# Second pair's 1/rms by bit shift and refinements on VectorE, whole-tile output stores, a split last tile

## Chip, core and metric

The kernel runs on one core of a Trainium2 chip. The metric is the device time of one execution in microseconds (us), as the median of several runs. The engines are named as the profile names them: PE (TensorE matmul), PEld (its weight loads), DVE (VectorE), ACT (ScalarE), POOL (GpSimd), SP (SyncE, which here issues nearly all DMAs; its queue is SPq).

## What is computed

Memory-compressed attention for 8 batches x 8 heads x 576 positions x 64 dimensions with 32 memory slots, and behind it an RMS norm and a gated feed-forward layer over 4608 tokens (512 -> 1536 -> 512).

```python
a = softmax(phi, axis=2)                          # 576 x 32 per head
k_m, v_m = a.T @ k, a.T @ v                       # 32 x 64 per head
x = softmax(q @ k_m.T / sqrt(64)) @ v_m           # then heads side by side: 4608 x 512
xn = x / sqrt(mean(x * x, axis=-1) + 1e-6) * rms_g
g = xn @ w_gate
out = (g * sigmoid(g) * (xn @ w_val)) @ w_out
```

q, k, v and phi are float32, the three weight matrices arrive as 8-byte floats, and the output is float32, 4608 x 512.

## The kernel before

The 8 batches are worked in 4 pairs. The kernel never forms x @ w: it multiplies v_m into the weights first (`vp`, tokens then enter through the 32-slot attention weights), so that one unit of work is small. Where float32 accuracy is wanted from a matmul, an operand is split into a high part and a low remainder (`xh`/`xl`, `ath`/`atl`, `hh`/`hl`, `oh`/`ol`) and three products are added: high x high, high x low, low x high. The high part is a cast on ACT, the remainder a subtraction on POOL or DVE.

**First stage (about 0 to 130 us).** For each batch phi is exponentiated, k and v are compressed (`kvp`), turned and normalized; for pairs 0 and 1 q is loaded, scores `S` and their softmax `a` are formed. `x_steps` then prepares the tokens of a pair: `a` is turned (`tp`, `at`), the norm's sum of squares comes from a small product with the v_m Gram matrix (`xp`, `ssq`, lines 275 to 293), and `fin` (lines 302 to 328) makes 1/rms from it, a 128x9 tile `rinv`. `fin` has two ways, chosen by `PRM["LN"]`: a pair whose number is below LN takes ln and exp on ACT (lines 312 and 313) and one refinement step on DVE; the others take an integer shift and a multiply-add on DVE (lines 316 and 319) and three refinement steps (lines 324 to 326, each three 128x9 instructions). With LN=2 pairs 0 and 1 go by ln and exp, pairs 2 and 3 by the shift. Behind `fin` come three groups of steps per pair: `rinv` is spread over partitions by PE (`rp`, line 238, for pair 1 in a buffer of the two that `po` uses too), DVE multiplies it into `at` (line 246), and ACT and POOL split `at` into `ath` and `atl` (lines 266 and 267). For pair 1 these last steps are put off into the second stage (`x_tail`).

**Second stage (from about 130 us).** 48 steps; the first 24 belong to pairs 0 and 1, the last 24 to pairs 2 and 3. Step i makes `vp` (12 matmuls, line 546) and splits it into `xh`, `xl` (lines 558 and 559), then the gate and value products `pg` and `pv` for its two batches and for two groups of token tiles (line 586), Silu of `pg` on ACT (`sg`, line 594), the product `hf` on DVE (line 595) and its split `hh`, `hl` (lines 613 and 614). After every second step (`out_steps`), for each of 9 token tiles t, 6 matmuls of 128x512 make `po` (line 1120); the first unit copies it into `acc` on ACT (line 1125), later ones add it on DVE (line 1128), and after the last unit the tile is stored by two DMAs of 64 rows each, one per batch of the pair (line 1132). So there are two bursts of stores: pairs 0 and 1 in the middle of the kernel (about 484 to 545 us) and pairs 2 and 3 at its end. During the first 24 steps the weights are converted from 8-byte floats with integer instructions on DVE (lines 413 to 443, `ex` and `mi`) and helpers on ACT and POOL, and pairs 2 and 3 get their attention. In the second half `vp` of pairs 2 and 3 is formed for both at once (`vq`, line 1059), split into `sh` and `sl` (lines 1083 and 1084) and sent in pieces of 32 rows to the places of `xh` and `xl` by DMA (line 1102); `sl` and `sh` get new values only when those DMAs have read them.

**Order.** Every step has a due time from the table `PRM` (in units of a first-stage clock, later in steps). All steps are sorted by it and written out; a scheduler with a model of the engines then fixes the order of each engine's queue. Each engine works through its queue in order. ACT must hold the table that has the function it is to run: an ACT_TABLE_LOAD stands wherever the next function needs another one. In the trace a load stands ahead of Silu, of ln and of exp wherever the function before was another of the three, save for pair 0's norm, which needs none.

Of the kernel before, what the change touches and what calls it, by code (L numbers as in the profile page):

```python
# [8 lines left out]
F32 = mybir.dt.float32  # L9
# [4 lines left out]
ALU = mybir.AluOpType  # L14
# [19 lines left out]
    POST=[-0.351, 1.753, 3.361, 9.334, 15.437, 18.292],
    P1=4.425,
    PREP=[4.415, 7.26, 7.26, 7.26, 20.861],
    PD=[1.16, 10.918, 7.968, 18.215, 7.667, 0.808],
    EXP=[-5.547, 10.093, -0.851, 3.808, 8.158, 5.953],
    ES=1.713,
    PH=[10.189, 16.336, 43.784, 73.222, 98.48, 135.656],  # L40
    S_AT=[32.811, 49.336, 51.299, 66.888, 103.621, 110.389, 116.081, 123.226],
    KD=[-25.933, -115.469, -42.204, -7.345, -6.094, -11.232, -0.175, -2.269, -27.578, -16.354, -20.47, -8.311,
        -12.025, -12.235, -27.337, -21.619, -19.41, -32.053, -14.0, -25.731, -11.785, -19.02, -8.155, -10.419,
# [37 lines left out]
    XN=[-0.287, -0.179, -0.049, 0.046, 0.258, 0.5, 0.652, 0.838, 0.858],
    LV=[19.704, 21.121, 20.046, 22.191],
    VD=[42.193, 5.807, 18.26, 22.229],
    U=[[-1.593, -1.385, -1.385, -1.17, -0.987, -0.894], [-1.558, -1.498, -1.292, -1.023, -1.023, -0.981],
        [-1.863, -1.411, -1.203, -0.927, -0.927, 0.553]],
    RL=[-1.987, -3.598, -5.966],
# [22 lines left out]
def kernel(  # L109
# [87 lines left out]
    def x_steps(pr, a, psum_t, psum_x, fetch=None, psum_r=None):  # L197
# [104 lines left out]
        def fin():  # L302
# [53 lines left out]
    raw, wsplit, wosplit, halves = {}, {}, {}, {}  # L356
# [39 lines left out]
    urgent = []  # L396
# [110 lines left out]
    NS = (NP // G) * NU * G * 2  # L507
    vw, vp_, whole, hsplit, accs, fourth = {}, {}, {}, {}, {}, []

    def mixed(i):  # L510
        return i >= NS // 2 + 2 * G

    def where(i):

        ps_, r = divmod(i, NU * G * 2)
        u, r = divmod(r, G * 2)
        pi, f = divmod(r, 2)
        if mixed(i):
            pi, f = f, pi
        return ps_, u, ps_ * G + pi, 2 * u + f  # L520
# [103 lines left out]
    with ExitStack() as c1:  # L624
# [3 lines left out]
        ps = c1.enter_context(tc.tile_pool(name="ps1", bufs=2, space=PSUM, reuse_waits="tile"))  # L628
# [412 lines left out]
    ps = ctx.enter_context(tc.tile_pool(name="ps2", bufs=2, space=PSUM, reuse_waits="tile"))  # L1041
# [64 lines left out]
    def out_steps(i):  # L1106

        ps_, u, pr, j = where(i)

        def f(t):  # L1110
            def g():
                gi = 0 if t < GROUPS[1][0] else 1
                po = ps.tile([P, 512], F32, tag="o", name=f"po{i}_{t}")
                m = 0
                for s in (i - 2 if mixed(i) else i - 1, i):
                    hh, hl = hsplit[s, gi]
                    oh, ol = wosplit[ps_ * NJ + where(s)[3]]
                    tt = t - GROUPS[gi][0]
                    for l, r in ((hh, oh), (hh, ol), (hl, oh)):
                        nc.tensor.matmul(po, l[:, tt, :], r, start=(m == 0), stop=(m == 5))  # L1120
                        m += 1
                key = pr % G, t
                if u == 0:
                    accs[key] = sb.tile([P, 512], F32, tag=f"acc{key[0]}_{t}", name=f"acc{pr}_{t}")
                    nc.scalar.copy(accs[key], po)
                else:
                    urgent.append(
                        nc.vector.tensor_tensor(out=accs[key], in0=po, in1=accs[key], op=ALU.add).ins  # L1128
                    )
                if u == NU - 1:  # L1130
                    for b in range(2):
                        nc.sync.dma_start(
                            out[(2 * pr + b) * S:(2 * pr + b + 1) * S].rearrange("(p c) d -> p c d", c=NT)[:, t, :],
                            accs[key][64 * b:64 * b + 64, :],
                        )
            return g
        return [f(t) for t in range(NT)]
# [119 lines left out]
    for i in range(NS):  # L1257
        ps_, u, pr, j = where(i)
# [21 lines left out]
    for a, (kind, n, p, e) in enumerate(items):  # L1280
        c = convert(kind, n)
# [46 lines left out]
```

## Time and profile before

| | |
|---|---|
| median of 3 runs | 855.59 us (855.2, 855.59, 857.08) |
| the profiled execution, its time | 850.64 us |
| its span, first to last instruction | 848.9 us (1.7 us less) |
| mean granted TensorE clock | 0.989 |
| PE busy | 812.3 us, 96% of the span |
| DVE, ACT, POOL busy | 537.0, 403.7, 322.9 us |
| chain that ended last | PE 74%, DVE 9%, DMA 5%, ACT 3%, issue 3%, POOL 3%, SPq 2% |
| output stores | 72 DMAs of 128.0 KB, 2.4 us to landing |

A row of the timeline gives the start in us from the span's beginning, the duration, the engine, the line, the operation, out<-in with shapes, how many instructions are merged into it, and in square brackets how long the engine stood idle before it and what released it. A row of a window table gives the length of the window, then for each engine its busy time in it with the number of instructions, and the granted PE clock, the DMA share and GB/s at the end. The profiled execution is 4.95 us shorter than the median of the timed runs; the profile does not say why.

### The profile page before, as it was taken

Reading aid. Unit: us, or ns where it says so; the run is one execution under the profiler, and the core shown is the slowest. Engines: PE = TensorE matmul, PEld = TensorE weight load, DVE = VectorE, ACT = ScalarE, POOL = GpSimd, SP = SyncE. Lnnn points to the kernel's source line nnn. Section 1 sums busy time; section 2 is a strip of 40 time slices with the busy share of each in tenths; the row PEclk is TensorE's granted clock in tenths of the full one; section 3 lists DMA queues with packets and bytes.
Section 4 is the critical chain, followed back from the end, with each engine's and each line's share of the span. In section 5 each row is a group of like instructions: output and inputs, shape, how many; then the busy total and the mean of one; then the engine's idle time right before and its main releaser. Section 6 shows DMA issues by size and latency. Waiting matters only on the chain.

```text
span 848.9 us, 16232 instructions
## 1 busy us (share of the span) xinstructions
PE 812.3 (96%) x6234; PEld 731.9 (86%) x6234; DVE 537.0 (63%) x940; ACT 403.7 (48%) x731; POOL 322.9 (38%) x279
## 2 busy tenths in 40 slices
PE   5989997999999999999999989999999999999997
PEld 4878886889989889988989888899999999999996
DVE  5697868876678898979889546312354454444434
ACT  2767647687565465656454423354333223232220
POOL 3565746734444563643544512411212122121220
PEclk9889999999999999999999999999999999999999
DMA  9997525545343543743534567806736357264437
GB/s 335 364 383 271 201 72 152 149 117 153 115 119 96 167 124 78 189 132 104 150 111 130 176 144 198 239 15 168 180 94 179 77 149 199 59 153 88 100 100 174
DMA packets 99493, 131.62 MB, mean 155 GB/s; under 512 B 42324, under 2 KB 61784, under 8 KB 99416
## 3 DMA queue, kind: packets, MB, share of 16 engines
q1 hardware_dynamic: 99416, 130.59, 54.6%
q8 instruction: 49, 0.80, 0.4%
q14 instruction: 28, 0.23, 0.1%
HBM read 73.93 MB, written 31.46 MB: 124 GB/s over the span
## 4 chain that ended last, share of the span: by engine, by line
PE 74%; DVE 9%; DMA 5%; ACT 3%; issue 3%; POOL 3%; SPq 2%; ACTq 0%; POOLq 0%; DVEq 0%
PE po L1120 31%; PE pg L586 14%; PE pv L586 14%; PE vp L546 3%; PE vq L1059 3%; PE kvp L787 2%; SPq L1102 1%; DVE xl L559 1%; DMA kv_0x<-in_k_dram 1%; DVE mi L438 1%; DVE ex L413 1%; DVE ex L416 1%; PE S L1199 1%; PE xp L280 1%; ACT xh L558 1%
## 5 line engine op out<-in xcount | busy, mean ns | idle before, releaser
L614 POOL TENSOR_TENSOR hl<-hf,hh 128x512 fp32r<-128x512 f32 (+1 forms) x86 | 124.5, 1449 | 285.7 <-ACT hh L613 285.6
L1128 DVE TENSOR_TENSOR acc<-po,acc 128x512 f32<-128x512 f32 x180 | 123.5, 688 | 124.2 <-PE po L1120 123.5
L1120 PE MATMUL po<-oh,hh 128*128 128x512 f32 x387 | 154.1, 399 | 4.5 <-DVE at L246 1.9
L1120 PE MATMUL po<-ol,hh 128*128 128x512 f32 x387 | 153.3, 396 | 0.5 <-DMA ol<-od 0.5
L1120 PE MATMUL po<-oh,hl 128*128 128x512 f32 x387 | 151.5, 391 | 0.0
L595 DVE TENSOR_TENSOR hf<-pv,sg 128x320 f32<-128x320 f32 (+1 forms) x188 | 83.4, 452 | 88.4 <-PE pv L586 64.3
L594 ACT ACTIVATE sg<-pg 128x320 f32<-128x320 f32 (+1 forms) x188 | 76.6, 410 | 123.4 <-PE pg L586 115.2
L586 PE MATMUL pg<-ath,xh 128*128 128x320 f32 (+1 forms) x376 | 85.9, 301 | 3.9 <-ACT sg L594 3.6
L1120 PEld LDWEIGHTS po<-oh,hh 128*128 128x128 f32 x387 | 73.0, 189 | 16.9 <-DVE at L246 2.1
L1120 PEld LDWEIGHTS po<-oh,hl 128*128 128x128 f32 x387 | 73.0, 189 | 16.1
L586 PE MATMUL pg<-ath,xl 128*128 128x256 f32 (+1 forms) x376 | 83.8, 297 | 0.7 <-DMA xl<-sl 0.7
L613 ACT CAST hh<-hf 128x512 fp32r<-128x512 f32 (+1 forms) x86 | 57.4, 672 | 55.2 <-DVE hf L595 37.6
L586 PE MATMUL pv<-ath,xl 128*128 128x256 f32 (+1 forms) x376 | 82.9, 296 | 0.0
L586 PE MATMUL pg<-atl,xh 128*128 128x256 f32 (+1 forms) x376 | 82.9, 297 | 0.0
L586 PE MATMUL pv<-ath,xh 128*128 128x320 f32 (+1 forms) x376 | 82.2, 298 | 0.4 <-DVE hf L595 0.3
L586 PE MATMUL pv<-atl,xh 128*128 128x256 f32 (+1 forms) x376 | 81.6, 296 | 0.0
L1120 PEld LDWEIGHTS po<-ol,hh 128*128 128x128 f32 x387 | 73.1, 189 | 9.0 <-DMA ol<-od 0.7
L462 POOL TENSOR_TENSOR w<-mi,ex 128x512 f32<-128x512 f32 x34 | 43.9, 1290 | 84.8 <-ACT mi L450 54.6
L586 PEld LDWEIGHTS pg<-ath,xh 128*128 128x128 f32 x376 | 62.6, 189 | 9.2 <-ACT sg L594 4.3
L559 DVE TENSOR_TENSOR xl<-vp,xh 64x1024 fp32r<-64x1024 f32 x48 | 58.5, 1219 | 16.4 <-ACT xh L558 15.6
L586 PEld LDWEIGHTS pv<-ath,xh 128*128 128x128 f32 x376 | 61.6, 189 | 3.6 <-DVE hf L595 0.9
L586 PEld LDWEIGHTS pg<-ath,xl 128*128 128x128 f32 x376 | 62.2, 190 | 2.8 <-DMA xl<-sl 0.9
(163 smaller groups left out, 1519.7 us busy)
## 6 DMA issues: line engine op xcount, KB each, us to landing
xh<-sh SPq DMA_DIRECT2D x96, 128.0 KB, 3.7
xl<-sl SPq DMA_DIRECT2D x80, 128.0 KB, 3.1
out_dram<-acc SPq DMA_DIRECT2D x72, 128.0 KB, 2.4
raw<-in_moe_w_gate_dram SPq DMA_DIRECT2D x12, 512.0 KB, 4.0
raw<-in_moe_w_val_dram SPq DMA_DIRECT2D x12, 512.0 KB, 3.8
raw<-in_moe_w_out_dram SPq DMA_DIRECT2D x12, 512.0 KB, 4.0
wd<-whl SPq DMA_DIRECT2D x24, 256.0 KB, 3.8
whl<-wd SPq DMA_DIRECT2D x12, 512.0 KB, 5.3
```

What stands on the lines that cost most here:

```text
L462: (nc.gpsimd if on_pool else V).tensor_tensor(out=d["w"], in0=m, in1=ex, op=ALU.mult)
L546: nc.tensor.matmul(vp[:, cc, e, :], lhs(l), r[:, 2 * cc + e, :], start=(n == 0), stop=(n == 2),)
L559: urgent.append(nc.vector.tensor_tensor(out=xl[rows], in0=src, in1=xh[rows].bitcast(F32), op=ALU.subtract).ins)
L586: nc.tensor.matmul(pt[:, :N], l[cc][:, b, half * P:half * P + P], r[:, cc, b, t0:t0 + n, :].rearrange("p t x -> p (t x)"), start=(m == 0), ...
L594: nc.scalar.activation(sg[:, :N], pg[:, :N], AF.Silu)
L595: urgent.append(nc.vector.tensor_tensor(out=hf[:, :, b, :], in0=pv[:, :N].rearrange("p (t x) -> p t x", x=64), in1=sg[:, :N].rearrange("p ...
L613: nc.scalar.copy(hh, hv)
L614: nc.gpsimd.tensor_tensor(out=hl, in0=hv, in1=hh.bitcast(F32), op=ALU.subtract)
L787: nc.tensor.matmul(kvp[64 * par:64 * par + 64, cc, 0:128], e_bd[j][:, hp, c, :], st["kv", b, hp][:, :, 64 * c:64 * c + 64], start=(c == 0) ...
L1059: nc.tensor.matmul(vp[:, h, e, :], vall[a][:, cc, k:k + 4, :].rearrange("p q m -> p (q m)"), w, start=(a == 0), stop=(a == 1),)
L1120: nc.tensor.matmul(po, l[:, tt, :], r, start=(m == 0), stop=(m == 5))
L1128: nc.vector.tensor_tensor(out=accs[key], in0=po, in1=accs[key], op=ALU.add).ins
```

## The change

Three edits, and a table fitted anew around them.

1. `LN` goes from 2 to 1: pair 1 takes the shift and three refinements on DVE; its ln and exp on ACT go. Only pair 0 keeps them.
2. An output tile is stored by one DMA of 128 rows for both batches of the pair, not by two of 64.
3. The last tile of the last step is made in two halves of 256 columns: 6 + 6 matmuls of 128x256, two adds, two stores; the first half's store is issued by ACT, the second's by SP.
4. Some 25 entries of `PRM` move (due times of loads, steps and copies), most by under 1 unit.

```diff
-    LN=2,
+    LN=1,
...
-    KP=0.885,
+    KP=0.826,
...
-    X_AT=[101.408, 161.722],
+    X_AT=[101.408, 160.333],
...
-                po = ps.tile([P, 512], F32, tag="o", name=f"po{i}_{t}")
...
+                acc = accs[key]
+                ends = 2 if i == NS - 1 and t == NT - 1 else 1
+                for e in range(ends):
+                    cols = slice(e * 512 // ends, (e + 1) * 512 // ends)
+                    po = ps.tile([P, 512], F32, tag="o", name=f"po{i}_{t}_{e}")[:, cols]
...
+                            nc.tensor.matmul(po, l[:, tt, :], r[:, cols], start=(m == 0), stop=(m == 5))
...
-                    for b in range(2):
-                        nc.sync.dma_start(
-                            out[(2 * pr + b) * S:(2 * pr + b + 1) * S].rearrange("(p c) d -> p c d", c=NT)[:, t, :],
-                            accs[key][64 * b:64 * b + 64, :],
+                    if u == NU - 1:
+                        (nc.scalar if e + 1 < ends else nc.sync).dma_start(
+                            out[2 * pr * S:(2 * pr + 2) * S].rearrange("(p c) d -> p c d", c=NT)[:, t, cols],
+                            acc[:, cols],
                         )
```

**ACT, where pair 1's norm ends** (`gram` is the last Gram copy, `sg_00` the first Silu of step 1). Before:

```order
L859 COPY gram_1764<-kvt_1768 128x128
L312 ACT_TABLE_LOAD
L312 ACTIVATE rinv_72<-m_1861 128x9
L613 CAST hh_0_1925<-hf_0_1729 128x512
L613 CAST hh_1_1934<-hf_1_1807 128x640
L313 ACT_TABLE_LOAD
L313 ACTIVATE rinv_72<-rinv_72 128x9
L558 CAST xh_1952<-vp_1938 64x2x2x256
L476 CAST oh_2030<-w_0_1912 128x512
L594 ACT_TABLE_LOAD
L594 ACTIVATE sg_00_1995<-pg_00_1981 128x256
```

Now:

```order
L859 COPY gram_1766<-kvt_1773 128x128
L613 CAST hh_0_1931<-hf_0_1735 128x512
L613 CAST hh_1_1940<-hf_1_1809 128x640
L558 CAST xh_1963<-vp_1945 64x2x2x256
L594 ACTIVATE sg_00_2004<-pg_00_1990 128x256
```

The ln, the exp and three table loads are gone, and the cast of `oh` now stands behind the first Silu.

**DVE at the same place**, from the first instruction of pair 1's `fin` to the multiplication of `rinv` into `at`. Before:

```order
L322 TENSOR_SCALAR m_1861<-m_1861 128x9
L413 TENSOR_SCALAR ex_1_1914<-raw_1747 128x512
L438 TENSOR_SCALAR mi_1_1919<-raw_1747 128x512
L324 TENSOR_TENSOR u_1864<-rinv_72 128x9
L416 TENSOR_SCALAR ex_1_1914<-ex_1_1914 128x512
L443 SCALAR_TENSOR_TENSOR mi_1_1919<-raw_1747,mi_1_1919 128x512
L325 TENSOR_TENSOR u_1864<-u_1864,m_1861 128x9
L559 TENSOR_TENSOR xl_1953<-vp_1938,xh_1952 64x2x2x256
L595 TENSOR_TENSOR hf_0_1980<-pv_00_1982,sg_00_1995 128x4x64
L326 SCALAR_TENSOR_TENSOR rinv_72<-u_1864,rinv_72 128x9
```

Now, behind the shift, the multiply-add and two whole refinements:

```order
L324 TENSOR_TENSOR u_1851<-rinv_72 128x9
L413 TENSOR_SCALAR ex_1_1920<-raw_1752 128x512
L438 TENSOR_SCALAR mi_1_1925<-raw_1752 128x512
L325 TENSOR_TENSOR u_1851<-u_1851,m_1848 128x9
L416 TENSOR_SCALAR ex_1_1920<-ex_1_1920 128x512
L443 SCALAR_TENSOR_TENSOR mi_1_1925<-raw_1752,mi_1_1925 128x512
L559 TENSOR_TENSOR xl_1964<-vp_1945,xh_1963 64x2x2x256
L326 SCALAR_TENSOR_TENSOR rinv_72<-u_1851,rinv_72 128x9
L595 TENSOR_TENSOR hf_0_1989<-pv_00_1991,sg_00_2004 128x4x64
L595 TENSOR_TENSOR hf_0_1989<-pv_01_2008,sg_01_2021 128x4x64
L430 SCALAR_TENSOR_TENSOR ex_1_1920<-raw_1752,ex_1_1920 128x512
L246 TENSOR_TENSOR at_1566<-at_1566,rp_0_1973 128x1024
```

Eight 128x9 instructions are added to the chain; the second `xl` and a `hf` that stood ahead of the first multiplication into `at` (line 246) now stand behind it. On PE the spreading of `rinv` (`rp_0`, `rp_4`) moves ahead of the six `pv_10` matmuls of step 1.

**SP in the first burst of stores** (`sl1x` to `xl` are the sends of line 1102; `acc0_t` are the tiles of pair 0). Before:

```order
L1132 DMA out_0_dram<-acc0_2_2224 64x512 x2
L1132 DMA out_0_dram<-acc0_3_2272 64x512 x2
L1102 DMA xl26_6106<-sl12_10_5992 32x2x256
L1102 DMA xl26_6106<-sl12_11_6050 32x2x256
L1102 DMA xl26_6106<-sl12_00_5991 32x2x256
L1132 DMA out_0_dram<-acc0_4_2322 64x512 x2
L1102 DMA xl26_6106<-sl12_01_6049 32x2x256
```

Now:

```order
L1102 DMA xl26_6106<-sl12_10_5994 32x2x256
L1102 DMA xl26_6106<-sl12_11_6052 32x2x256
L1102 DMA xl26_6106<-sl12_00_5993 32x2x256
L1136 DMA out_0_dram<-acc0_2_2224 128x512
L1102 DMA xl26_6106<-sl12_01_6051 32x2x256
L1136 DMA out_0_dram<-acc0_3_2271 128x512
```

Half as many store DMAs stand in the queue, and those of tiles 2, 3 and 4 come later among the sends. Further on, the loads of `whl` move from behind two dozen sends to right behind the store of tile 5. On PE the 8 matmuls of `vq_1` that wait for `sl` move ahead of five `pv_11`, two `xp` and four `tp` matmuls. In the first stage SP's load of `q0_0` and that of the batch-2 tile `kv2_0` change places.

More of the change, by code (lines that the diff above doesn't have):

```diff
@@ L24 @@
     V0S=[-7.546, 0.266, 0.444],
-    G0=[3.08, 8.562, 9.611, 9.895],
-    V1=[11.959, 17.008, 23.081],
+    G0=[3.08, 8.562, 8.562, 9.895],
+    V1=[11.62, 17.198, 23.271],
     E1=1,
-    LN=2,
-    R1=[1.117, 1.117, 1.171, 1.171, 1.388, 1.633, 1.633, 1.633, 1.633],
+    LN=1,
+    R1=[1.117, 1.117, 1.171, 1.171, 1.618, 1.633, 1.633, 1.633, 1.633],
     KB=4,
     QB=3,
-    K_AT=[13.077, 14.811, 42.175, 65.611, 100.792, 122.017, 151.093, 167.171],
-    KP=0.885,
-    POST=[-0.351, 1.753, 3.361, 9.334, 15.437, 18.292],
-    P1=4.425,
+    K_AT=[13.077, 14.811, 42.381, 65.611, 100.792, 122.017, 151.093, 167.171],
+    KP=0.826,
+    POST=[-0.351, 1.753, 3.361, 9.334, 15.559, 18.292],
+    P1=4.352,
     PREP=[4.415, 7.26, 7.26, 7.26, 20.861],
     PD=[1.16, 10.918, 7.968, 18.215, 7.667, 0.808],
-    EXP=[-5.547, 10.093, -0.851, 3.808, 8.158, 5.953],
+    EXP=[-6.258, 10.634, -0.851, 3.808, 7.78, 5.953],
     ES=1.713,
-    PH=[10.189, 16.336, 43.784, 73.222, 98.48, 135.656],
+    PH=[9.276, 16.336, 43.784, 73.222, 98.48, 135.656],
     S_AT=[32.811, 49.336, 51.299, 66.888, 103.621, 110.389, 116.081, 123.226],
@@ L47 @@
     QL=3.814,
-    OL=4.061,
-    QO=[-0.958, 5.498, -1.004, -0.051, -0.269, 3.82],
-    SO=[11.73, 17.082, 17.082, 24.847],
-    X_AT=[101.408, 161.722],
+    OL=4.974,
+    QO=[-0.958, 5.498, -1.004, -0.109, -0.269, 3.848],
+    SO=[11.695, 17.082, 17.082, 24.847],
+    X_AT=[101.408, 160.333],
     XP=2.11,
@@ L67 @@
     RP=1.163,
-    GV=[0.204, 0.21, 0.449, 0.743, 0.743, 0.854],
+    GV=[0.204, 0.21, 0.449, 0.743, 0.743, 0.839],
     VW=[-0.087, -0.015, 0.011],
@@ L72 @@
     PRE=[-0.629, 0.024, 0.147, 1.342, 2.043, 2.557],
-    PRE0=[-2.562, 0.061, 0.845, 1.122, 1.647, 2.014],
+    PRE0=[-2.641, 0.0, 0.766, 1.043, 1.568, 1.935],
     PI=0.121,
@@ L76 @@
     SU=[1.877, 4.574, 5.755, 6.56, 9.726, 13.02, 13.928, 15.536],
-    AO=[0.305, 0.305, 0.305, 0.305, 0.388, 0.423, 0.581, 0.581, 0.597, 0.643, 0.659, 0.856, 0.946, 1.397],
+    AO=[0.305, 0.305, 0.305, 0.312, 0.388, 0.423, 0.581, 0.581, 0.597, 0.643, 0.659, 0.856, 0.946, 1.397],
     XB=[17.199, 22.73],
@@ L80 @@
     XM=[21.739, 25.092],
[L81 to L86, printed above, removed]
+    XN=[-0.287, -0.179, -0.049, 0.046, 0.149, 0.5, 0.652, 0.838, 0.858],
+    LV=[19.704, 21.048, 20.046, 22.191],
+    VD=[42.193, 5.807, 18.26, 20.884],
+    U=[[-1.591, -1.383, -1.383, -1.168, -0.985, -0.892], [-1.558, -1.498, -1.292, -1.023, -1.023, -0.981],
+        [-1.863, -1.411, -1.203, -0.874, -0.874, 0.553]],
+    RL=[-1.987, -3.572, -5.966],
     RW=[0.968, 0.323],
@@ L1112, in g @@
                 gi = 0 if t < GROUPS[1][0] else 1
-                po = ps.tile([P, 512], F32, tag="o", name=f"po{i}_{t}")
[L1114 to L1121, printed above, removed]
                 key = pr % G, t
@@ L1124, in g @@
                     accs[key] = sb.tile([P, 512], F32, tag=f"acc{key[0]}_{t}", name=f"acc{pr}_{t}")
[L1125 to L1130, printed above, removed]
-                    for b in range(2):
-                        nc.sync.dma_start(
-                            out[(2 * pr + b) * S:(2 * pr + b + 1) * S].rearrange("(p c) d -> p c d", c=NT)[:, t, :],
-                            accs[key][64 * b:64 * b + 64, :],
+                acc = accs[key]
[3 more added lines that the diff above has]
+                    po = ps.tile([P, 512], F32, tag="o", name=f"po{i}_{t}_{e}")[:, cols]
+                    m = 0
+                    for s in (i - 2 if mixed(i) else i - 1, i):
+                        hh, hl = hsplit[s, gi]
+                        oh, ol = wosplit[ps_ * NJ + where(s)[3]]
+                        tt = t - GROUPS[gi][0]
+                        for l, r in ((hh, oh), (hh, ol), (hl, oh)):
+                            nc.tensor.matmul(po, l[:, tt, :], r[:, cols], start=(m == 0), stop=(m == 5))
+                            m += 1
+                    if u == 0:
+                        nc.scalar.copy(acc, po)
+                    else:
+                        urgent.append(
+                            nc.vector.tensor_tensor(out=acc[:, cols], in0=po, in1=acc[:, cols], op=ALU.add).ins
+                        )
+                    if u == NU - 1:
+                        (nc.scalar if e + 1 < ends else nc.sync).dma_start(
+                            out[2 * pr * S:(2 * pr + 2) * S].rearrange("(p c) d -> p c d", c=NT)[:, t, cols],
+                            acc[:, cols],
                         )
```

## The prediction

> **What bounds the kernel now.** I read the totals first, then the busy time by stage, then the timeline of the engines in the stages where PE stands idle.
>
> ```profile
> PE 812.3 (96%) x6234; PEld 731.9 (86%) x6234; DVE 537.0 (63%) x940; ACT 403.7 (48%) x731; POOL 322.9 (38%) x279
> 125.00:150.00 25.00, 18.90 (x160) 16.80 (x157) 20.30 (x41) 19.63 (x37) 15.80 (x12) 0.93 0.46 129
> 150.00:175.00 25.00, 23.52 (x175) 20.92 (x174) 22.15 (x32) 18.34 (x33) 18.28 (x15) 1.00 0.54 147
> 500.00:600.00 100.00, 95.93 (x591) 86.02 (x589) 38.83 (x89) 40.42 (x78) 25.02 (x19) 1.00 0.59 154
> ```
>
> PE is busy for 812.3 of 848.9 us, so only its 36.6 us of idle time and its slow stretches can be won. In each window the first number after the length is PE: it idles 6.1 us of 125 to 150 and 4.07 us of 500 to 600. These are the two places that the edits touch, and the end is the third.
>
> Pair 1's norm, on ACT, then PE:
>
> ```profile
> 129.80 1.28 ACT L312 ACT_TABLE_LOAD   x1
> 132.95 1.28 ACT L313 ACT_TABLE_LOAD   x1
> 135.89 1.28 ACT L594 ACT_TABLE_LOAD   x1
> 137.62 0.56 PE L586 MATMUL pg<-ath,xh 128*128 128x320 f32 x2 [2.62 <-ACT sg L594]
> 139.48 0.46 PE L586 MATMUL pv<-ath,xh 128*128 128x320 f32 x2
> 140.36 1.03 PE L238 MATMUL rp<-ident,rinv 128*128 128x128 f32 x8
> 146.43 0.60 PE L1120 MATMUL po<-oh,hh 128*128 128x512 f32 x1 [1.85 <-DVE at L246]
> 143.30:146.70 3.40, 1.54 (x12) 1.34 (x11) 3.40 (x5) 1.92 (x4) 3.03 (x3) 1.00 0.59 205
> 146.70:150.10 3.40, 3.40 (x12) 2.82 (x12) 3.07 (x6) 3.40 (x8) 3.00 (x2) 0.50 0.00 0
> ```
>
> Three table loads of 1.28 us stand ahead of the first Silu, and PE waits 2.62 us for that Silu. Then it waits 1.85 us, because `po` takes a buffer from which DVE has yet to read `rp`. In the 3.4 us with that wait PE is busy for 1.54, and in the next 3.4 us its granted clock is 0.50, which costs 1.7 us more. So this stage loses 2.62 + 1.85 + 1.7 = 6.2 us that `fin` of pair 1 causes.
>
> **Edit 1, the norm.** The Silu comes early without the loads: ACT sheds 3 x 1.28 = 3.8 us there, and the ln and exp, and the 2.62 us go. What is late next is `rinv`, now ahead of `pv_10` on PE. PE reaches `rp` at 137.62 - 2.62 + 1.86 (the twelve `pg`, 137.62 to 139.48) = 136.9. When is `rinv` there? The chain by the shift is in this trace, for pairs 2 and 3:
>
> ```profile
> 131.17 0.17 DVE L304 TENSOR_SCALAR m<-ssq 128x9 f32<-128x9 f32 x1
> 134.49 0.89 DVE L324 TENSOR_TENSOR u<-rinv 128x9 f32<-128x9 f32 x1 [1.82 <-ACT rinv L313]
> 136.24 1.22 DVE L325 TENSOR_TENSOR u<-u,m 128x9 f32<-128x9 f32 x1
> 138.85 0.15 DVE L326 SCALAR_TENSOR_TENSOR rinv<-u,rinv 128x9 f32<-128x9 f32 x1
> 132.39 2.97 POOL L614 TENSOR_TENSOR hl<-hf,hh 128x512 fp32r<-128x512 f32 x2 [1.44 <-ACT hh L613]
> 135.95 1.49 POOL L477 TENSOR_TENSOR ol<-w,oh 128x512 fp32r<-128x512 f32 x1 [0.59 <-ACT oh L476]
> 457.71 0.23 DVE L304 TENSOR_SCALAR m<-ssq 128x9 f32<-128x9 f32 x1
> 465.96 0.16 DVE L326 SCALAR_TENSOR_TENSOR rinv<-u,rinv 128x9 f32<-128x9 f32 x1
> 522.37 0.16 DVE L304 TENSOR_SCALAR m<-ssq 128x9 f32<-128x9 f32 x1
> 527.11 0.16 DVE L326 SCALAR_TENSOR_TENSOR rinv<-u,rinv 128x9 f32<-128x9 f32 x1
> ```
>
> Pair 1 takes 139.0 - 131.17 = 7.8 us by ln and exp. Pair 3, with POOL standing idle beside it, takes 527.27 - 522.37 = 4.9 us by the shift, pair 2, with POOL at work for much of the time, 466.12 - 457.71 = 8.4, each with other DVE work in between. These are the ends. POOL is busy here too (`hl`, `ol`), and the order puts five larger instructions into the chain, so I take 7.0: `rinv` at 138.2. The new wait at `rp` is 1.3 us.
>
> Behind `rp` the first `at` multiplication starts 1.27 us later (140.36 to 141.63 now):
>
> ```profile
> 141.63 1.21 DVE L246 TENSOR_TENSOR at<-at,rp 128x1024 f32<-128x1024 f32 x1
> ...
> 145.17 1.21 DVE L246 TENSOR_TENSOR at<-at,rp 128x1024 f32<-128x1024 f32 x1
> ```
>
> Today 2.3 us of weight conversion lie between the two multiplications (142.84 to 145.17); the new order has one `xl` there, which I take to last as long as a multiplication, 1.21. So the second ends at 138.2 + 1.27 + 3 x 1.21 = 143.1. PE's own work from `rp` to `po` is 4.2 us today (140.36 to 144.58, where the wait of 1.85 begins); `pv_10` comes in with 0.88 (139.48 to 140.36), and two of the next step's first products now fall behind `po`. So PE is there at 138.2 + 4.2 + 0.88 = 143.3 or a little less, as early as DVE's result, and since both are rough I leave 0.3 us of wait. Waits of 2.62 + 1.85 = 4.47 us become 1.6: 2.9 us won. No 3.4 us stretch is then half idle, so the 0.50 stretch goes too: 1.7 us. Of these 4.6 us I give 1.7 back: DVE is busy for 22.15 of 25 us right after, and gets 8 more instructions of 0.17 to 0.2 us (1.6 us in sum). **Edit 1: -2.9 us**, between -0.5 (chain as long as pair 2's, the half clock stays) and -6.2.
>
> On the half clock a rule of the Trainium skill speaks against me. TensorE: Matmul & The Clock Gate, "What's actually happening", has PE fall to half clock after at least one idle window of a free-running 3.4 us grid. Here a window with 1.54 us of work already did it, so trace and page differ and the trace decides; by the page the slow stretch would not come from this wait and could stay, and the sum would be 1.7 us smaller.
>
> **Edit 2, the stores.** SP's queue, and who waits for it:
>
> ```profile
> 479.50 0.62 SPq L483 DMA_DIRECT2D od<-ol  x1
> 484.82 2.47 SPq L1132 DMA_DIRECT2D out_dram<-acc  x4
> 489.42 3.54 SPq L1132 DMA_DIRECT2D out_dram<-acc  x4
> 495.06 1.18 SPq L1132 DMA_DIRECT2D out_dram<-acc  x2
> 496.29 3.25 SPq L1102 DMA_DIRECT2D xl<-sl  x5
> 500.44 0.69 DVE L1084 TENSOR_TENSOR sl<-vq,sh 128x512 fp32r<-128x512 f32 x1 [2.55 <-issue]
> 502.53 1.22 PE L1059 MATMUL vq<-whl,va 128*128 128x256 f32 x8 [2.23 <-DVE sl L1084]
> 516.45 0.35 PE L586 MATMUL pg<-ath,xl 128*128 128x256 f32 x1 [0.72 <-DMA xl<-sl]
> 528.76 0.98 PE L1059 MATMUL vq<-whl,va 128*128 128x256 f32 x6 [0.27 <-DMA whl<-wd]
> ```
>
> A store of 64 rows costs SP about 0.6 us, and so does the 128-row store of `ol` at 479.50: the price is per DMA. Ten stores stand ahead of the last sends of `sl` today, four in the new order, so these go 6 x 0.6 = 3.6 us earlier. `sl` waits for the sends to land (its release is not named by the trace; sends of `sl` right before it are the likeliest), PE waits for `sl`. PE comes to `vq` about 1.5 us earlier by the new order, so 2.1 of the 2.23 us go, and the two smaller DMA waits of 0.72 and 0.27 with them: **-3.1 us**, between -0.5 (`sl` waits for something else) and -4.07 (all idle time of that window). In the last burst nothing on PE waits for SP.
>
> **Edit 3, the end.**
>
> ```profile
> L1132 SPq DMA_DIRECT2D out_dram<-acc x72: 466/587/1612, 484.8 to 845.5; - x72
> 844.23 0.69 DVE L1128 TENSOR_TENSOR acc<-po,acc 128x512 f32<-128x512 f32 x1 [0.67 <-PE po L1120]
> 138.52 0.40 DVE L595 TENSOR_TENSOR hf<-pv,sg 128x256 f32<-128x256 f32 x1
> DMA to landing us min/median/max: 2.2/2.4/6.0
> ```
>
> Behind the last matmul come an add of 0.69 us, two issues of 0.47 to 0.59 and a landing of 2.2 to 2.4. An add of 256 columns takes 0.40, and one issue is left: 0.29 + 0.57 = **-0.85 us**. The matmuls keep their columns, the first half's add and store hide behind the second half's matmuls, and ACT has nothing else to do there. If they do not hide, 0.3 is left; if the smaller store lands sooner, 1.2.
>
> **The table.** Elsewhere the re-fitted due times swap neighbours in the queues and move single loads by a few places; I find no swap there that puts a late result ahead of a waiting engine. I put 0 for the table, plus or minus 1.5 us, the idle time that PE has in 150 to 175 today (25 - 23.52).
>
> **The sum** is -2.9 - 3.1 - 0.85 = -6.85 us, that is 843.8 for the profiled execution of 850.64 us. The timed runs lie 4.95 us above that execution, for a reason that the profile does not show; taking the difference from their median gives 855.59 - 6.85 = **848.7 us**.
>
> **Rivals.** *POOL holds the chain.* In the rows above the refinement's `u` ends at 135.38, POOL's `hl` at 135.36, the next at 137.46, POOL's `ol` at 137.44: a 128x9 product that meets a POOL instruction lasts 0.89 to 1.22 us instead of 0.17. The change puts nine such products into a stretch where POOL works. If four of them are caught, the chain takes 4 us more than pair 3's, `rinv` comes at 140, PE waits 3 us at `rp` for the 2.62 that it saved, and with the work behind DVE late edit 1 gives about 0.2: 855.59 - 0.2 - 3.1 - 0.85 = 851.4. For it: pair 2's 8.4 us. Against: POOL has only three or four instructions in this stretch, and each can catch one product at most. The Trainium skill, SBUF — State Buffer, "Who interferes with whom", has the same as a rule: a DVE instruction with two SBUF inputs contends with a GpSimd instruction that reads SBUF, and whoever comes second waits it out. The trace agrees (135.38 against 135.36).
>
> *The stores were not what held SP.* If `sl` waits for PE's or DVE's own progress, edit 2 gives 0.5 instead of 3.1: 851.3. For it: the trace calls 2.55 us of that wait "issue", with no releaser. Both rivals at once give 854.0.
>
> *Slower: all nine products are caught.* Nine times 1.06 us (the mean of 0.89 and 1.22) and some 4 us of the other work in it make a chain of 13.7 us and `rinv` at 144.9; PE then idles for 8.0 us on end at `rp`, 3.8 more than the 4.47 of today with the 0.3 behind it, and falls into one or two more stretches at half clock (1.7 us each). Edit 1 then costs 5.5 to 7.2, the others give 3.95: 858.0. The sign turns once the chain passes about 12 us. No chain in the trace is longer than 8.4.
>
> *It does nothing.* If DVE and POOL, nearly full from 140 to 175, set the pace there and SP's queue is refilled by the sends, about 855 is left.
>
> **Chances.** The forecast 0.62, POOL holding the chain 0.15, stores not binding 0.10, both or no effect 0.08, slower 0.05. Within 0.2% (1.7 us, about what timing this kernel can tell from no change) lie the last part of "both" and "no effect": faster 0.87, same 0.08, slower 0.05. The range 843.5 to 854.5 takes in the rivals up to both at once, and downwards the upper bounds of edits 1 and 2 (another 3.3 + 1.0 us) with part of the table's 1.5.
>
> **What would show it.** Right: no table load between the first Silu and the first exp of the later pairs' attention, no wait of PE for `sg` there, a wait at `rp` near 1.3 us, no 0.50 stretch near 147; 36 or 37 store issues of about 0.6 us, no wait of 2 us for `sl` near 500; an end 0.85 us shorter behind the last matmul. Wrong: `u` rows of over 1 us and a chain of over 8 us; PE idle of over 3 us in 500 to 600; or new idle time of over 1.5 us in stages that the edits do not touch.

## The result, and the profile after

The changed kernel takes 864.88 us (median of 4, 864.63 to 866.2) against 856.34 of the kernel before; the ratio is 1.011, 95% interval 1.0086 to 1.0134, so it is slower by 1.1%, which on 856.34 is some 9.4 us (7.4 to 11.5). The two medians alone lie 8.5 us apart. The forecast was 848.7. The profiled execution took 864.63 us, its span is 862.9.

Windows of the changed kernel (columns as in the prediction: after the length PE, PEld, DVE, ACT, POOL, granted clock, DMA share, GB/s):

```profile
125.00:150.00 25.00, 19.84 (x220) 18.68 (x216) 22.19 (x49) 12.81 (x26) 11.20 (x10) 0.93 0.43 120
500.00:600.00 100.00, 92.78 (x557) 82.89 (x556) 37.56 (x87) 34.84 (x69) 24.26 (x18) 0.97 0.53 147
143.57:146.99 3.42, 3.42 (x16) 3.42 (x15) 3.37 (x5) 3.25 (x7) 2.27 (x2) 0.50 0.60 178
157.23:160.64 3.41, 3.41 (x12) 2.91 (x13) 2.85 (x3) 1.75 (x4) 2.65 (x3) 0.50 0.50 159
519.04:525.87 6.83, 5.57 (x18) 4.92 (x19) 0.49 (x1) 0.00 (x0) 0.00 (x0) 0.50 0.60 148
```

PE is idle for 7.2 us of 500 to 600, where it was for 4.07 before and the forecast left about 1 (4.07 less 3.1). And there are two stretches at half clock at and behind the norm and a double one from 519 us. In 125 to 150 PE is busy for 19.84 us, against 18.90 before, at the same granted clock of 0.93.

A window at the same time no longer holds the same work. So I also timed the same work: the start of the matmul that stands at the same share of all matmul columns in both traces, with the marks at the times that the shown profile of before has. In us:

| trace | 0-76 | 76-125 | 125-176 | 176-493 | 493-550 | 550-840 | 840-end | span |
|---|---|---|---|---|---|---|---|---|
| before, the profile shown | 76.0 | 49.0 | 51.0 | 317.0 | 57.0 | 290.0 | 8.9 | 848.9 |
| before, another execution | 79.9 | 49.0 | 52.2 | 316.7 | 56.3 | 290.0 | 8.9 | 853.0 |
| after | 80.2 | 47.3 | 55.5 | 319.4 | 62.8 | 290.0 | 7.7 | 862.9 |

The second execution of before is 3.9 us longer than the first in the first stretch, and differs by 1.2 us or less in each of the others: the profile that I predicted from was an early finisher. Against the second one the changed kernel loses 3.3 us where the norm of pair 1 stands, 2.7 from 176 to 493, 6.5 in the first burst of stores, and gains 1.7 and 1.2: 9.9 us by stages, 9.4 by the timed runs.

**The norm.** DVE and POOL from the last sum of squares to `rinv`, and PE behind it:

```profile
133.62 1.30 POOL L462 TENSOR_TENSOR w<-mi,ex 128x512 f32<-128x512 f32 x1
134.88 2.84 POOL L614 TENSOR_TENSOR hl<-hf,hh 128x512 fp32r<-128x512 f32 x2
137.66 1.31 POOL L477 TENSOR_TENSOR ol<-w,oh 128x512 fp32r<-128x512 f32 x1
...
134.44 0.52 DVE L304 TENSOR_SCALAR m<-ssq 128x9 f32<-128x9 f32 x1
134.99 1.22 DVE L307 TENSOR_SCALAR m<-m 128x9 f32<-128x9 f32 x1
136.24 1.50 DVE L316 TENSOR_SCALAR rinv<-m 128x9 int32<-128x9 int32 x1
137.78 1.22 DVE L319 TENSOR_SCALAR rinv<-rinv 128x9 int32<-128x9 int32 x1
139.03 0.17 DVE L324 TENSOR_TENSOR u<-rinv 128x9 f32<-128x9 f32 x1
143.16 0.15 DVE L326 SCALAR_TENSOR_TENSOR rinv<-u,rinv 128x9 f32<-128x9 f32 x1
...
143.37 1.81 PE L238 MATMUL rp<-ident,rinv 128*128 128x128 f32 x8 [3.24 <-DVE rinv L326]
```

POOL works without a break from 133.62 to 138.97, and the first four steps of the chain end when one of its instructions ends: 134.96 with `w` (134.92), 136.21 and 137.74 with the two `hl` that the row merges (137.72), 139.00 with `ol` (138.97). They last 4.46 us in sum (0.52 + 1.22 + 1.50 + 1.22) where 0.17 is the time of a step that meets nothing. The other ten steps come behind POOL and cost 0.15 to 0.17 each. Between the last three of them stand five larger instructions (two `ex`, two `mi` and an `xl`), which fill 140.34 to 143.16. The chain takes 143.31 - 134.44 = 8.9 us and PE waits 3.24 us at `rp`.

**The stores.** SP's queue at the end of the first burst, what PE waits for, and in the view of the DMA issues the median time to landing of what was issued from 509.9 on:

```profile
509.31 0.54 SPq L1136 DMA_DIRECT2D out_dram<-acc  x1
509.94 0.91 SPq L503 DMA_DIRECT2D whl<-wd  x2
510.96 2.85 SPq L1102 DMA_DIRECT2D xh<-sh  x4
...
520.30 0.77 PE L586 MATMUL pg<-ath,xh 128*128 128x256 f32 x2 [4.65 <-DMA xh<-sh]
...
whl<-wd SPq DMA_DIRECT2D x2, 512.0 KB, 7.1
xh<-sh SPq DMA_DIRECT2D x4, 128.0 KB, 7.6
```

The wait of `vq` for `sl`, 2.23 us before, is gone as forecast. But two loads of 512 KB now stand ahead of the sends of `sh`, and these land 7.6 us after their issue. Before, the loads were issued at 522.15, behind the sends, and those landed in 2.4 us (four of them, issued from 514.99; the four ahead of these took 2.6):

```profile
522.15 1.02 SPq L503 DMA_DIRECT2D whl<-wd  x2
xh<-sh SPq DMA_DIRECT2D x4, 128.0 KB, 2.4
```

**The end.** The last add starts at 859.69 and the span ends 3.2 us later; before it was 844.23 and 4.7:

```profile
859.69 0.42 DVE L1133 TENSOR_TENSOR acc<-po,acc 128x256 f32<-128x256 f32 x1 [0.62 <-PE po L1127]
```

### The profile page after: what moved, and what is told of

It is laid out like the page before. It is cut to its first block, busy times and chain, and to the rows that moved or that the text cites. A ratio compares the mean times of both kernels' runs of the same rounds, so it can differ in the third digit from the quotient of the medians.

```text
span 862.9 us, 16222 instructions
## 1 busy us (share of the span) xinstructions
PE 817.6 (95%) x6240; PEld 736.7 (85%) x6240; DVE 539.7 (63%) x949; ACT 401.6 (47%) x726; POOL 323.2 (37%) x279
## 3 DMA queue, kind: packets, MB, share of 16 engines
q1 hardware_dynamic: 98840, 130.45, 52.3%
## 4 chain that ended last, share of the span: by engine, by line
PE 77%; DVE 11%; DMA 4%; ACT 3%; issue 3%; SPq 1%; POOL 0%; DVEq 0%; ACTq 0%; POOLq 0%
PE po L1127 31%; PE pv L586 15%; PE pg L586 15%; PE vp L546 3%; PE kvp L787 3%; PE vq L1059 2%; DMA phi<-in_phi_dram 2%; DVE xl L559 1%; DVE mi L438 1%; DVE mi L443 1%; PE xp L280 1%; DVE hf L595 1%; PE gv L586 1%; DMA xh<-sh 1%; PE tp L218 1%
## 5 line engine op out<-in xcount | busy, mean ns | idle before, releaser
L1133 DVE TENSOR_TENSOR acc<-po,acc 128x512 f32<-128x512 f32 (+1 forms) x181 | 123.7, 685 | 131.7 <-PE po L1127 131.1
L586 PE MATMUL pv<-ath,xh 128*128 128x320 f32 (+1 forms) x376 | 84.0, 302 | 2.0 <-DVE hf L595 1.5
L586 PE MATMUL pv<-ath,xl 128*128 128x256 f32 (+1 forms) x376 | 81.7, 297 | 0.0
L462 POOL TENSOR_TENSOR w<-mi,ex 128x512 f32<-128x512 f32 x34 | 43.9, 1291 | 86.3 <-ACT mi L450 56.1
L586 PEld LDWEIGHTS pg<-atl,xh 128*128 128x128 f32 x376 | 62.3, 191 | 2.0
```

The lines of the kernel that those rows point to most:

```text
L462: (nc.gpsimd if on_pool else V).tensor_tensor(out=d["w"], in0=m, in1=ex, op=ALU.mult)
L586: nc.tensor.matmul(pt[:, :N], l[cc][:, b, half * P:half * P + P], r[:, cc, b, t0:t0 + n, :].rearrange("p t x -> p (t x)"), start=(m == 0), ...
L1133: nc.vector.tensor_tensor(out=acc[:, cols], in0=po, in1=acc[:, cols], op=ALU.add).ins
```

## The experiments

My theory from these traces: the stores cost by the loads that slip ahead of the sends; the norm costs by POOL's hold on its chain; the table has a share in the first stage. The rivals stand in the expectations. Each kernel ran 12 times beside the kernel before; ratios are to that, each with its 95% interval. The stage times below are made as those above, from the one profiled execution of each, so they carry its chance: the profile of the table alone is the slowest of its 12 runs (865.52 us), that of the stores alone the fastest (852.86).

**The parts alone.** The kernel before once more; `LN=1` alone; one store of 128 rows alone; the table alone (with `LN=2`).

```diff
# norm alone            # stores alone: the change's own lines, with ends = 1
-    LN=2,              # table alone: every other changed entry of PRM
+    LN=1,
```

> The kernel before, unchanged, for what its own executions differ by. Its profiled execution of 850.64 us lies 5 us under its timed runs, so a single profile may flatter it. If the half clock follows a grid of 3.4 us whose position against the program is left to chance, runs of the same program show between 2 and 6 slow windows and granted clocks of 0.98 to 0.99, and the median is again 855 to 857. If the first profile was the typical one, the clock is 0.989 in all and the median near 851.

> Edit 1 alone: LN=1, nothing else. Theory (POOL holds the chain): the first four 128x9 steps of pair 1's shift meet POOL's hl and ol and last over 1 us each, the chain takes 8 to 9 us, PE waits about 3 us at rp in place of the 2.62 and 1.85 us of before, and the half-clock window stays: 0 to +2 us, 856 to 858. My prediction's step would give -2.9 us, about 853. Rival (the re-fitted table caused the late chain, not the edit): chain of 7 us or less here.

> Edit 2 alone: one store of 128 rows instead of two of 64, the table of before. In its order SP issues the two loads of whl for the unit after next 23 places earlier than before, ahead of 8 sends of sh and their sl. Theory (the loads hold the sends in the queue): the sends of sh land 7 to 8 us after their issue instead of 2.4, PE waits 4 to 5 us for xh near 515 us, one or two half-clock windows follow, and of the 2.9 us of waits that go nothing is left: +3 to +5 us, 859 to 861. My prediction's step: -3.1 us, 853.

> The re-fitted table alone, with LN=2, 64-row stores and the undivided last tile. Theory: the lag of 3.4 us that the changed kernel has by 97 us of its first stage comes from the table (later kv load, later k tile): +2 to +3.5 us, 858 to 860. Rival: the first stage differs by that much from run to run, and the table alone is within 1.5 us of before, as my prediction had it. Rival that the table alone makes the whole loss: +8 us, 864.

| run | median | ratio | 0-76 | 125-176 | 176-493 | 493-550 | end |
|---|---|---|---|---|---|---|---|
| before again | 856.98 | 1.000 (0.998 to 1.002) | 79.9 | 52.2 | 316.7 | 56.3 | 8.9 |
| norm alone | 856.72 | 0.9999 (0.9977 to 1.002) | 80.3 | 54.1 | 317.0 | 56.1 | 8.9 |
| stores alone | 857.52 | 1.0007 (0.9986 to 1.0028) | 76.5 | 51.0 | 317.0 | 59.7 | 7.9 |
| table alone | 860.61 | 1.0051 (1.003 to 1.0072) | 81.7 | 56.4 | 322.3 | 57.2 | 8.9 |

None gains, and the table alone loses 4.4 us, but not in the first stage as I had it: in 125 to 176 and 176 to 493. The stores alone cost 0.6 us (-1.2 to 2.4) where I had expected 3 to 5. In their run the loads have slipped too and PE waits:

```profile
509.62 0.77 PE L586 MATMUL pg<-ath,xh 128*128 128x256 f32 x2 [3.11 <-DMA xh<-sh]
```

So it is the store edit that moves the loads, with the due times of before. The norm's run shows the chain at its longest, 136.28 to 148.91 or 12.6 us, with steps that wait for POOL at both ends of it:

```profile
136.28 1.02 DVE L304 TENSOR_SCALAR m<-ssq 128x9 f32<-128x9 f32 x1
137.34 1.50 DVE L307 TENSOR_SCALAR m<-m 128x9 f32<-128x9 f32 x1
138.87 0.17 DVE L316 TENSOR_SCALAR rinv<-m 128x9 int32<-128x9 int32 x1
147.70 1.21 DVE L326 SCALAR_TENSOR_TENSOR rinv<-u,rinv 128x9 f32<-128x9 f32 x1
...
138.87 1.32 POOL L477 TENSOR_TENSOR ol<-w,oh 128x512 fp32r<-128x512 f32 x1
147.59 1.29 POOL L477 TENSOR_TENSOR ol<-w,oh 128x512 fp32r<-128x512 f32 x1
```

The shift at 138.87 meets no instruction that has already begun and costs 0.17. My slower rival priced a chain of 13.7 us at 5.5 to 7.2 us; one of 12.6 costs 2 to 3 in its stage, and nothing that the timed runs can tell, since in this order PE has the rest of step 1's products and the next `vp` to do ahead of `rp`: `rp` starts at 149.29, without a wait for `rinv`.

**The loads put back.** A second set: the divided tile alone; 128-row stores with the two loads held behind the last send; the changed kernel with the same hold; all three edits with the table of before, without the hold.

```diff
-        for a in range(2):
-            nc.sync.dma_start(t[a].bitcast(F32), src[:, a])
+        with tc.issue_after(sent[-1]) if kind == 0 and n == 15 else nullcontext():
+            for a in range(2):
+                nc.sync.dma_start(t[a].bitcast(F32), src[:, a])
```

> Edit 3 alone: the last tile in two halves of 256 columns, each stored by two DMAs of 64 rows, the table of before. My prediction's step: -0.85 us (-0.3 to -1.2); the distance from the last matmul's start to the end of the span is the number to read, since single executions of the kernel before spread over 852 to 859 us. Rival: the half stores land no sooner and cost two issues more, 0 to +0.5 us.

> 128-row stores alone, with the two loads of whl held where SP had them before: behind the last send of the unit before. Theory (the loads that slipped ahead cost the 3.1 us wait for xh): that wait is gone, the sends of sh land in about 2.4 us, and the stage 490 to 565 is 3 to 4 us shorter than in the run with the stores alone. Against before: -1 to -3 us if the stores are what sl waited for, 0 if not. Rival (a store of 256 KB in one piece blocks the ring): the wait for xh stays at 2 to 3 us.

> The changed kernel with the same two loads held behind the sends; nothing else differs. Theory: of its loss of 9 us the 4.65 us wait for xh and the half-clock windows behind it go, 5 to 6.5 us: 858 to 860. Rival (the loads only happen to stand there, the table costs it all): unchanged, 864 to 866.

> All three edits with the due times of before: the re-fitted table is left out. Theory (costs add up: norm 0, stores +0.6, split -0.85, table +4.4): 855 to 857, that is 8 us under the changed kernel, of which the table is the half. Rival (the edits interact with each other, not with the table): 860 to 864.

| run | median | ratio | 125-176 | 176-493 | 493-550 | end |
|---|---|---|---|---|---|---|
| divided tile alone | 857.49 | 0.9999 (0.9978 to 1.0021) | 52.2 | 316.9 | 59.0 | 8.3 |
| stores, loads held | 853.87 | 0.9976 (0.9959 to 0.9992) | 51.9 | 317.0 | 56.5 | 7.9 |
| after, loads held | 857.79 | 1.0025 (1.0006 to 1.0044) | 54.5 | 319.8 | 56.9 | 7.7 |
| all edits, old table | 859.51 | 1.0037 (1.0021 to 1.0054) | 54.3 | 317.0 | 61.9 | 7.7 |

Holding two DMAs takes the changed kernel from 1.011 to 1.0025, 7 us, and the stage from 62.8 to 56.9. With the stores alone it is 1.0007 to 0.9976, 2.7 us. The rival that the bigger store blocks the sends falls: the stores are the same in both, and with the loads held no DMA is among PE's waits from 490 to 560. All edits with the old table came to 859.51 us, not to the 855 to 857 that the sum of the parts gives: the loads slip there too, and PE waits 3.70 us for `xh`. What PE waits for from 490 to 560 in the changed kernel with the hold:

```profile
PE rp L238 <- DVE rinv L326: 1.3, 1, 1.3
PE xp L275 <- DVE acc L1135: 1.2, 1, 1.2
PE xp L275 <- ACT at L228: 0.9, 1, 0.9
PE pv L588 <- DVE hf L597: 0.5, 1, 0.5
```

No DMA and no `sl` is among them, and yet these 3.9 us are as much as the 4.0 of the same view of before (2.2 for `sl`, 0.7, 0.5, 0.3 and 0.3): pair 3's own norm and its copies are late next. The divided tile's 59.0 comes with 3.4 us at half clock in that stretch; its edit lies 290 us further on, so I take this for chance.

**The norm freed of POOL.** A third set, with the loads held in all. In the first and third, fin's `m`, shifted word and `u` of pair 1 lie in PSUM, so that only `u<-rinv,rinv` still takes all its operands from SBUF.

```diff
-            m = persist.tile([P, NT], F32, tag="m", name=f"m{pr}")
+            m = m2 = persist.tile([P, NT], F32, tag="m", name=f"m{pr}")
+            if pr == 1:
+                ft = psum_x(f"fin{pr}")
+                m = ft[:, :NT]
...
+            u = ft[:, 32:32 + NT] if pr == 1 else persist.tile([P, NT], F32, tag="u", name=f"u{pr}")
...
+                rp = ft[:, 16:16 + NT].bitcast(I32) if pr == 1 else ri
...
-            nc.vector.tensor_scalar(out=m, in0=m, scalar1=-0.5, scalar2=None, op0=ALU.mult)
+            nc.vector.tensor_scalar(out=m2, in0=m, scalar1=-0.5, scalar2=None, op0=ALU.mult)
```

> The changed kernel with the loads of whl held, and pair 1's norm with its intermediate tiles (m, the shifted word, u) in PSUM; only r times r still takes its inputs from SBUF alone. Theory (a VectorE step that reads and writes SBUF alone waits out POOL's instruction, one with an operand in PSUM does not): the first four steps of fin last 0.15 to 0.3 us instead of 0.52 to 1.50, the chain takes 4 to 6 us instead of 8.9, the wait at rp falls from 3.2 to under 1 us, and the time is 1 to 3 us under the run with the loads held alone: 855 to 857. Rival (the steps are long for another reason, their own cost or the queue): the chain stays over 8 us and the time at 857.8.

> Edits 2 and 3 with the due times of before, the loads of whl held, and the norm by ln and exp (LN=2). The run with 128-row stores and the loads held lies 2.0 us under before; the divided tile adds 0.2 us of gain at the end, since the end was 7.9 us by the stores alone and 7.7 by both. Theory: 853 to 854. Rival (that gain was chance, 0 from the middle burst): 855.

> The same with LN=1 and the norm's intermediates in PSUM: all three edits, the due times of before, both costs mended. Theory: the chain of 12.6 us of the norm alone with this table becomes 5 to 7, the waits of 2.1 and 2.3 us at pg and rp shrink to 2 in sum, 850 to 853. Rival (DVE is full in 125 to 175, so the added instructions cost what the loads gave): 853 to 855.

> The changed kernel with LN back at 2 and the loads of whl held: table, stores and divided tile without the norm. The table alone with LN=2 cost 4.4 us and lost most of it in 137 to 176 us (45.5 against 39 to 40). Theory (the table was fitted to LN=1 and fits nothing else): 857 to 859, no better than with the norm. Rival (the norm costs in any table): 853 to 855.

| run | median | ratio | 125-176 | 176-493 |
|---|---|---|---|---|
| after, PSUM | 857.95 | 1.0026 (1.0006 to 1.0046) | 56.8 | 316.8 |
| old table, LN=2 | 853.52 | 0.9969 (0.995 to 0.9988) | 52.3 | 316.9 |
| old table, LN=1, PSUM | 858.73 | 1.0031 (1.0009 to 1.0053) | 58.2 | 317.2 |
| after, LN=2 | 859.74 | 1.0041 (1.0017 to 1.0064) | 55.1 | 320.9 |

The steps of the first run, with POOL at work on two `hl` from 134.02 to 136.79:

```profile
133.65 0.17 DVE L307 TENSOR_SCALAR fin<-ssq 128x9 f32<-128x9 f32 x1
134.55 0.79 DVE L328 TENSOR_TENSOR fin<-rinv 128x9 f32<-128x9 f32 x1
135.79 1.04 DVE L328 TENSOR_TENSOR fin<-rinv 128x9 f32<-128x9 f32 x1
136.86 0.18 DVE L329 TENSOR_TENSOR fin<-fin,m 128x9 f32<-128x9 f32 x1
140.36 0.16 DVE L330 SCALAR_TENSOR_TENSOR rinv<-fin,rinv 128x9 f32<-128x9 f32 x1
...
134.02 2.77 POOL L620 TENSOR_TENSOR hl<-hf,hh 128x512 fp32r<-128x512 f32 x2
...
140.57 1.97 PE L238 MATMUL rp<-ident,rinv 128*128 128x128 f32 x8 [5.94 <-DVE rinv L330]
```

The mechanism holds: beside the same POOL work the steps with an operand in PSUM take 0.17 us and the one without takes 0.79 and 1.04. The chain falls to 6.9 us. The time doesn't fall: in the new order `rp` stands ahead of all of step 1's products, and PE, which came to it earlier, waits 5.94 us. The old table fares no better: 858.73 us where I had expected 850 to 853, with a wait of 5.7 us at `rp`. That the tile in PSUM also holds one of the buffers that `xp` uses may have a share in this; no run separates it. The PSUM run has the new table too, yet 176 to 493 takes 316.8 us in it, as before: what the table loses in that stage depends on what else is in the queues. The kernel with both edits to the stores, the loads held and ln and exp is the fastest of all, 0.9969; to the changed kernel that is 1.4% or some 12 us.

**Norm against table, and the norm without POOL.** A last pair, both with the old table and the loads held: the change's norm as it is; and every step with an operand in PSUM (`u` as r times m, then times r), with `rp` due behind the 12 products of step 1's first group.

```diff
-    R1=[1.117, 1.117, 1.171, 1.171, 1.388,
+    R1=[1.230, 1.230, 1.230, 1.230, 1.388,
...
-                nc.vector.tensor_tensor(out=u, in0=r, in1=r, op=ALU.mult)
-                nc.vector.tensor_tensor(out=u, in0=u, in1=m, op=ALU.mult)
+                nc.vector.tensor_tensor(out=u, in0=r, in1=m2 if pr == 1 else r, op=ALU.mult)
+                nc.vector.tensor_tensor(out=u, in0=u, in1=r if pr == 1 else m2, op=ALU.mult)
```

> All three edits with the due times of before and the loads of whl held; the norm as the change has it. Against the same kernel with LN=2 (853.5) it gives the norm's cost in this table, against the changed kernel with the loads held (857.8) the table's cost. Theory (the chain of 12.6 us and the waits behind it cost 3 to 5 us): 857 to 859, and the table then costs nothing beside the norm. Rival (the norm alone measured 0 against before, so it costs nothing here): 853 to 855, and the table costs 4.

> The same, but every step of pair 1's fin has one operand in PSUM (the word r is kept there, u is r times m and then times r), and the first four entries of R1 are 1.23 and not 1.117 to 1.171, so that PE has the 12 products of the first group of step 1 ahead of rp. Theory (POOL's hold and the place of rp on PE are what kept edit 1 from its gain): steps of 0.15 to 0.25 us, a chain of 5 to 6 us, a wait at rp under 1.5 us in place of 5.7, the stage 125 to 176 at 47 to 50 us and the time at 850 to 853. Rival (VectorE is full there and the next result is late by as much): the stage stays at 53 to 55 us and the time at 856 to 859.

The norm as it is: 856.2 us, ratio 1.0006 (0.9991 to 1.002), stage 125 to 176 in 54.3 us. Freed: 854.71 us, 0.9988 (0.9973 to 1.0003), 53.5 us, still over the 52.3 of ln and exp. The time lies between my theory (850 to 853) and the rival (856 to 859). DVE and PE of the freed one:

```profile
134.94 0.17 DVE L307 TENSOR_SCALAR fin<-ssq 128x9 f32<-128x9 f32 x1
136.46 1.33 DVE L418 TENSOR_SCALAR ex<-raw 128x512 int32<-128x512 int32 x1
137.72 0.16 DVE L329 TENSOR_TENSOR u<-fin,m 128x9 f32<-128x9 f32 x1
137.79 1.43 DVE L443 TENSOR_SCALAR mi<-raw 128x512 int32<-128x512 int32 x1
139.15 0.41 DVE L421 TENSOR_SCALAR ex<-ex 128x512 int32<-128x512 int32 x1
141.26 0.17 DVE L331 SCALAR_TENSOR_TENSOR rinv<-u,fin 128x9 f32<-128x9 f32 x1
...
141.57 1.06 PE L238 MATMUL rp<-ident,rinv 128*128 128x128 f32 x8 [2.81 <-DVE rinv L331]
145.17 0.90 PE L593 MATMUL pg<-ath,xh 128*128 128x320 f32 x2 [2.54 <-ACT sg L601]
```

All steps are at 0.17 and the chain still takes 6.5 us: the weight conversions between them read SBUF alone, and the first `ex` and the `mi` are held to 1.33 and 1.43 us, while POOL works (`ol` ends at 138.94); the same two lines take 0.43 each when they come again at 142.39 and 148.43. PE's larger waits there are 2.81 for `rinv`, 2.54 for `sg` and 1.8 for a `po` buffer, 7.1 us in sum, where the same kernel with ln and exp has 4.5 for `sg` and 0.5 for `po`. Two things differ from the norm as it is, the operands in PSUM and the place of `rp`. With PSUM and the early place of `rp` this table took 858.73 us, so the place counts, but no run moves `rp` alone.

## Why the prediction was wrong, step by step

By the ratios of the timed runs the loss adds up, each part put on top of those named ahead of it: the stores with the loads held -2.0 us, the divided tile -0.6, the norm 3.2, the table 1.6, and the two loads that slip ahead 7.3 (0.9976, 0.9969, 1.0006, 1.0025, 1.011), 9.4 us in sum. The intervals of these steps are 1.4 to 2.2 us to either side, that of the last is 2.6; so the divided tile and the table cannot be told from 0 here.

**Edit 2, -3.1 us: this step failed, and cost most.** Its premise held: a store costs SP one issue whatever its rows, fewer stand ahead of the sends, and the wait for `sl` went. What failed is the sentence on the table, "I find no swap there that puts a late result ahead of a waiting engine". The order that I had shown has the loads of `whl` "right behind the store of tile 5"; that swap was in front of me, and I priced only what left the queue, not what moved up in it. The runs show that price: 3.1 to 4.65 us of wait for `xh` and up to 6.8 us at half clock behind it, 2.7 us by the timed runs of the stores alone and 7 in the changed kernel. Why it is more there isn't settled: the wait is longer by 1.5 us and twice as much half clock follows it, but the intervals of the two differences, some 0.3% to either side, just overlap. With all edits and the old table the hold is again worth 2.7 us (1.0037 to 1.0006), so the larger price shows only together with the new table. And the gain itself was too large: with the loads held, the stage takes 56.9 us against 57.0 and 56.3 before, since other waits stand there instead (3.9 us for 4.0). The stores with the loads held gain 2.0 us by the timed runs, and 1.0 of these is at the end.

The Trainium skill, DMA: Bandwidth & Descriptors, "Queues, rings and completion order", says that each DMA engine takes the descriptors of a queue in their order. The trace agrees: behind two loads of 512 KB the sends land 7.6 us after issue, ahead of them 2.4.

**Edit 1, -2.9 us: this step failed too; with the due times of before it is wrong in sign.** The Silu's wait of 2.62 went, and so did that of `po`, as forecast. The chain took 8.9 us and not 7.0, and the wait at `rp` 3.24 and not 1.3. The mis-sized term is what POOL catches: I counted the products with two inputs, as in the rows of before, and took the steps with one input for free. In the changed kernel four of these were held, 4.46 us, and no product. My rival "POOL holds the chain" had the mechanism, `rinv` 3 us late, and its price for this edit (0.2 us gained) is nearer, but it went on with -3.1 of edit 2. "No 3.4 us stretch is then half idle" failed too: two at half clock follow, for one before. And the 1.7 us for that one belonged to the single execution that I read: in the second execution of before PE waits 1.84 us at the same `po` and is busy for 1.65 us of the 3.40 from 146.80 to 150.20, and the clock stays at 1.00 behind it. In its stage the edit costs 2 to 3 us; by timed runs it costs nothing alone (2 us either way) and 3.2 us (0.9969 to 1.0006) beside the other two edits. With the new table and the loads held, the kernel with the norm is 1.4 us faster than that with ln and exp (1.0041 to 1.0025), less than the intervals can tell from 0. With its steps freed of POOL it still gains nothing over ln and exp. What binds the stage then is argued, not shown: the 128x512 conversions stand between the steps on DVE, and two of them are still held.

The Trainium skill has the rule that I left out: SBUF — State Buffer, "Who interferes with whom", says beside the rule on two inputs that a tensor_scalar in a mode that uses both SBUF ports contends with GpSimd as well. The trace agrees: 1.22 and 1.50 us with `m` and the word in SBUF, 0.17 with them in PSUM.

**Edit 3, -0.85 us: right in kind.** The stretch from 840 on is 1.2 us shorter. Not all of it is the divided tile: whole-tile stores alone take 1.0 off, the divided tile alone 0.6. The issue that is spared, 0.47 to 0.59 us in the prediction's rows, is a part of that 1.0.

**The table, 0 with 1.5 either way.** With the norm and the loads held it costs 1.6 us (1.0006 to 1.0025, less than the intervals can tell from 0); without the norm 4.4 alone and 6.2 beside the other two edits (0.9969 to 1.0041). It gains 1.7 us in 76 to 125 in each of its runs and loses that or more behind 125. Norm and table together cost 4.8 us beside the other edits with the loads held (0.9969 to 1.0025), and how this splits depends on which of the two comes first: 3.2 and 1.6, or 6.2 and -1.4. So the table costs least beside `LN=1`. Which entries lose is open.

**The base.** The profile of 850.64 us is at the fast end of what the kernel before does (its timed runs went up to 859.9), mostly in its first 76 us. I took differences from the median, so this moved no term, but one profile hid how much of the half clock is chance.

## What to carry to other kernels

When a queue gets shorter, look at what moves up in it, not only at what leaves: here two large transfers that slipped ahead of small ones that an engine waits for cost 2.7 and 7 us. A chain of tiny VectorE steps is priced by what GpSimd does beside it and by what the order puts between its steps; PSUM operands take away the first, not the second. And a table of due times fitted to one set of edits says nothing of any one of them, so undo the parts singly and keep those that hold: here the whole-tile stores and the divided tile, with two loads held back.

## What the runs showed of the hardware

Each slow stretch of the clock lasts 3.4 us or a multiple of it, save where the span ends, and the same kernel has other ones in each execution: the two profiles of before have them at 20 to 27, 48 to 55 and 147 to 150 us, and at 17 to 21, 24 to 27, 48 to 55, 75 to 79 and 171 to 174. The first 76 us, the same work in all runs with the old table, take 76.0 to 81.1 us. So one profile settles nothing under some 5 us of this kernel, and a stage away from these stretches settles more than the sum. Nor does PE have to be idle for long: between the first two slow stretches of the changed kernel it is busy for 2.69 of 3.40 us. Nor does the busy share alone decide it: in the second execution of before 1.63 us of work in the 3.41 from 167.28 on is followed by half clock, 1.65 us in the 3.40 from 146.80 on is not.

```profile
20.70:24.10 3.40, 2.69 (x52) 2.44 (x53) 3.37 (x11) 2.97 (x3) 0.54 (x1) 1.00 0.66 241
```
